# A gated FFT and MLP mix: the second forward product merged into one 512-wide product, first pieces loaded in halves, and a new order of work

## The chip, the cores and the metric

The kernel runs on one core of a Trainium2 chip. Its time is the device time of one execution in microseconds; of several runs the median is given. The engines are TensorE (PE, with its weight loads as PEld), VectorE (DVE), ScalarE (ACT), GpSimd (POOL) and SyncE (SP); the queues of SP, ACT and POOL issue DMAs.

## The reference

For x of 2048 positions by 512 features, in float32:

```python
g = sigmoid((x * gate_w).sum(-1, keepdims=True))
a = irfft2(rfft2(x) * (w_r + 1j * w_i), s=(2048, 512))
b = gelu(x @ w1 + b1) @ w2 + b2          # 512 -> 1792 -> 512
out = g * a + (1 - g) * b
```

## The kernel before

**Number format.** Every matmul operand is split into a high and a low part (type fp32r, names ending in `h` and `l`): ACT or DVE casts the high part, DVE subtracts it to get the low one. A product is then three matmuls, high x high, low x high and high x low, summed in PSUM. All matmuls are issued at line 530, from the helper `mm`.

**The MLP.** The 2048 positions are four column groups c of 512, the 1792 hidden features fourteen groups f of 128. `mlp(half, c)` does seven of the f: the up product `ph` (12 matmuls of 512 columns, line 1105), gelu on ACT (1106), a split of the result into `g_..h` and `g_..l`, and the down product `po` over four output groups q (line 1137). For the very first tile, f=0 of c=0, the up product goes in two groups of 256 columns (lines 1093 to 1103), so that it can begin with two of four input pieces: x0 and x4, then x8 and x12. Input tiles are `xf` (x0, with the gate's weights behind it; issued by ACT, line 606) and `xr` (x4, x8, x12 and later ones; by SP, line 588). `split_1` makes `mxh` and `mxl` of them (649, 650). The weights are `war` and `wbr`, split into `wa..` and `wb..`.

**The FFT.** The 2048 positions are 16 residues j by 128 rows. For each j, `forward(j)` folds the 512 features into even and odd sums (`eo`, `cl`), splits them, multiplies them by a cosine and sine table `cf` (first forward product `pd`, per cosine and sine half c: two matmuls of 260 columns and two of 130), casts and subtracts the result into `xh` and `xl`, and multiplies those along the 128 rows by the table `tf` (second forward product `py`). Sixteen `Y[j]` are then combined by radix-4 steps on DVE, filtered, and transformed back (`pz`, `pa`). The outputs of both branches are weighted with the gate and added, partly by accumulating DMAs.

**The second forward product before.** The halves c = 0 and c = 1 have a PSUM tile of 258 columns each (line 747). For c = 1 the table is read 64 columns further on, for which ACT copies 64 of its columns behind its end (710). So there are six matmuls of 258 columns a group j. ACT copies the first tile to `pys` (757); DVE adds it to the second into `Y[j]` part 0 (758). Part 1 is the difference with its 64-partition halves swapped: for the first four j DVE writes both halves (767), for the twelve in `BY_ACT` DVE subtracts once (761) and ACT moves the halves (764).

**Start.** DVE clears a tile, eleven 512-wide matmuls on it keep PE busy (`warm`), ACT loads its function table (595), and the first DMAs go out: x0 by ACT; by SP the first weight, x4, x8 and x12, each in one piece of 256 KB.

**Order.** `add` makes a step for each instruction or small group, with engine, estimated cost and the tiles that it reads and writes. `schedule` (line 219) plays the steps through as a list schedule: on each engine the ready step with the least rank goes next, if its tiles find a slot (`slots`, `most`: at most three `py` tiles). The ranks come from the table `RANKS` (line 342), one a step. The steps are emitted in that order, so each engine's queue is fixed when the kernel is built, and runs in order.

Of the kernel before, what the change touches and what calls it, by code (L numbers as in the profile page):

```python
# [11 lines left out]
F32 = mybir.dt.float32  # L12
# [5 lines left out]
P = 128  # L18
# [97 lines left out]
SPARE = 0.4  # L116
LATE_X = 1
# [55 lines left out]
class Graph:  # L173
# [5 lines left out]
    def add(self, eng, cost, lag, emit, reads=(), writes=(), rank=1):  # L179
# [10 lines left out]
        for x in reads:  # L190
            b, ps = parts(x)
            for p in ps:
                if b.wrote[p] is not None:
                    deps.add(b.wrote[p])
                b.read[p].append(s)
            if b not in s.bufs:
                s.bufs.append(b)
# [258 lines left out]
def tile_kernel(ctx: ExitStack, tc: tile.TileContext, xt, w1, w2, b1, b2, x0g, wf, wrev, out, consts):  # L456
# [37 lines left out]
    def c_pe(n, k=1):  # L494
        return k * (n / 2400 + 0.0135) + 0.005
# [102 lines left out]
    def warm():  # L598
        for _ in range(11):
            mm(none.ap(), zero.ap(), bcast(zero.ap(), 4), True, True)  # L600
# [6 lines left out]
    for j in NORD[1:4]:  # L607
        XF[j] = load_x(j)
# [682 lines left out]
```

## Time and profile before

| what | value |
|---|---|
| median of 3 runs | 372.84 us (372.68 to 372.93) |
| profiled execution, span from first to last instruction | 370.8 us |
| time of a run outside such a span (372.84 - 370.8) | 2.04 us |
| granted TensorE clock, mean | 0.999 |
| PE matmuls | 1838 |
| DVE, ACT, POOL instructions | 691, 454, 54 |

The page gives the profiled execution's span and no other time of it, so times of runs are compared with spans by way of the 2.04 us. In the rows of the profile a group of instructions has its line, engine, operation, and output<-input tiles with buffer numbers left out; matmuls overlap, so the step from one start to the next is what a matmul costs PE, and its own duration is longer. A bracket at the end of a row holds the idle time of the engine before it, and what ended it. In rows by window, the columns are the window, its length, each engine's busy time with its number of instructions, the granted clock, the DMA engines' busy share, and GB/s.

### The profile page before, as it was taken

The numbers are of one execution on the slowest core, as the hardware profiler recorded it, in microseconds if no ns is written. First come the engines' busy times: TensorE is split into PE (matmuls) and PEld (weight loads), VectorE is DVE, ScalarE is ACT, GpSimd is POOL, SyncE is SP. The second block draws the span as 40 slices with busy tenths as digits, with TensorE's granted clock in tenths as the row PEclk, the third lists the DMA queues.
The fourth block names the chain that finished last, engine by engine and source line by source line (L and its number), as shares of the span: only waits on it lengthen the run. The fifth ranks groups of instructions, "written<-read, shape, count | busy, mean of one in ns | idle before, by whom it ended". The sixth has DMA issues, their size and how long they took to land.

```text
span 370.8 us, 5565 instructions
## 1 busy us (share of the span) xinstructions
PE 365.1 (98%) x1838; PEld 309.9 (84%) x1838; DVE 327.5 (88%) x691; ACT 229.6 (62%) x454; POOL 44.1 (12%) x54
## 2 busy tenths in 40 slices
PE   8999999999999999999999999999999999999995
PEld 6888888888888888888888888888888888888885
DVE  4999999999999789999999999588849696789996
ACT  5776587976678735375367213894697549457830
POOL 0000000000000002021032020001403222221031
PEclk9999999999999999999999999999999999999999
DMA  8962899425954216479289762318968999736268
GB/s 276 389 194 73 257 282 342 147 71 151 289 173 141 77 23 170 142 157 256 72 214 267 225 120 55 57 25 291 209 130 112 211 285 187 130 88 139 88 85 198
DMA packets 50868, 62.99 MB, mean 170 GB/s; under 512 B 4656, under 2 KB 31344, under 8 KB 50064
## 3 DMA queue, kind: packets, MB, share of 16 engines
q1 hardware_dynamic: 43496, 49.54, 41.3%
q0 software_dynamic: 7200, 12.85, 23.1%
q8 instruction: 14, 0.23, 0.2%
q10 hardware_dynamic: 144, 0.26, 0.2%
q14 instruction: 14, 0.11, 0.1%
HBM read 38.64 MB, written 23.73 MB: 168 GB/s over the span
## 4 chain that ended last, share of the span: by engine, by line
PE 95%; DVE 1%; DMA 1%; issue 0%; ACT 0%; SPq 0%; DVEq 0%
PE ph L530 41%; PE po L530 40%; PE pz L530 4%; PE pd L530 4%; PE py L530 3%; PE pa L530 3%; DMA xr<-in_xt 1%; DVE uv L1002 0%; DVE y L1021 0%; SPq L588 0%; DVE y L1024 0%; DVE mxl L650 0%; DVE o L1168 0%; ACT mxh L649 0%; ACT od L999 0%
## 5 line engine op out<-in xcount | busy, mean ns | idle before, releaser
L1106 ACT ACTIVATE ph<-ph,b1t 128x512 f32<-128x512 f32 x56 | 36.9, 659 | 41.5 <-PE ph L530 39.9
L949 ACT ACTIVATE sw<-y,al 64x512 f32<-64x512 f32 x32 | 23.0, 722 | 2.2 <-DVE y L812 1.6
L908 DVE TENSOR_TENSOR m<-y,wf 128x514 f32<-128x514 f32 x32 | 20.8, 689 | 0.2
L956 DVE SCALAR_TENSOR_TENSOR pq<-y,al,sw 128x256 f32<-128x256 f32 x32 | 14.4, 481 | 5.9 <-ACT sw L952 5.5
L521 POOL DMA_DIRECT2D bacc<-o x12 | 10.5, 877 | 73.2 <-ACT o L1155 60.2
L521 POOL DMA_DIRECT2D wa7l<-in_w x1 | 1.0, 1017 | 141.0 <-ACT wa7l L582 141.0
L1155 ACT ACTIVATE o<-po 128x512 f32<-128x512 f32 x12 | 7.1, 595 | 15.9 <-PE po L530 15.8
L1152 ACT ACTIVATE o<-po,b2t 128x512 f32<-128x512 f32 x16 | 10.7, 686 | 7.6 <-PE po L530 7.5
L1002 DVE TENSOR_TENSOR uv<-pa,od 128x512 f32<-128x512 f32 x16 | 10.6, 685 | 3.6 <-ACT od L999 3.5
L764 ACT ACTIVATE y<-pys 64x257 f32<-64x257 f32 x24 | 10.0, 418 | 5.2 <-DVE pys L761 4.8
L530 PE MATMUL pd<-cf,eoh 128*128 128x260 f32 x64 | 12.7, 285 | 0.0
L688 DVE TENSOR_TENSOR eo<-xr 128x256 f32<-128x256 f32 x30 | 12.0, 418 | 0.0
L530 PEld LDWEIGHTS pd<-cf,eoh 128*128 128x128 f32 x64 | 10.6, 189 | 1.5 <-issue 0.2
L999 ACT ACTIVATE od<-pa 128x512 f32<-128x512 f32 x8 | 4.8, 599 | 10.2 <-PE pa L530 9.9
L952 ACT ACTIVATE sw<-y 1x512 f32<-1x512 f32 x16 | 10.1, 629 | 0.4
L530 PE MATMUL pd<-cf,eol 128*128 128x130 f32 x64 | 10.3, 253 | 0.0
L702 DVE TENSOR_TENSOR xr<-eo 128x256 f32<-128x256 f32 x24 | 9.8, 418 | 0.1
L530 PEld LDWEIGHTS pd<-cf,eol 128*128 128x128 f32 x64 | 9.6, 189 | 0.1
L649 ACT ACTIVATE mxh<-xm 128x512 fp32r<-128x512 f32 x12 | 6.9, 623 | 3.7 <-PE ph L530 3.7
L650 DVE TENSOR_TENSOR mxl<-xm,mxh 128x512 fp32r<-128x512 f32 x12 | 7.8, 686 | 1.2 <-ACT mxh L649 1.2
L705 DVE TENSOR_TENSOR eol<-xr,eoh 128x512 fp32r<-128x512 f32 x12 | 8.3, 688 | 0.2
L1046 DVE SCALAR_TENSOR_TENSOR ba<-gb,ba 128x512 f32<-128x512 f32 x12 | 8.1, 685 | 0.3 <-DMA ba<-bacc 0.3
(713 smaller groups left out, 1353.6 us busy)
## 6 DMA issues: line engine op xcount, KB each, us to landing
wf<-in_wf SPq DMA_DIRECT2D x16, 257.0 KB, 4.9
bacc<-o SPq DMA_DIRECT2D x16, 256.0 KB, 3.3
xr<-in_xt SPq DMA_DIRECT2D x15, 256.0 KB, 3.5
war<-in_w SPq DMA_DIRECT2D x14, 256.0 KB, 3.5
wbr<-in_w SPq DMA_DIRECT2D x14, 256.0 KB, 3.5
xm<-in_xt SPq DMA_DIRECT2D x12, 256.0 KB, 4.3
bacc<-o POOLq DMA_DIRECT2D x12, 256.0 KB, 4.0
ba<-bacc SPq DMA_DIRECT2D x12, 256.0 KB, 3.2
```

What stands on the lines that cost most here:

```text
L521: return add("pool", kb / 150, 3.4, lambda: nc.gpsimd.dma_start(dst(), src(), accum_op=ALU.add), reads, writes, rank)
L530: pe.matmul(ps, w, x, start=start, stop=stop)
L688: v(lambda s=s, op=op: vec.tensor_tensor(eo.ap()[:, s], x.ap()[:, 0:2], x.ap()[:, 2:4], op=op), 256, [x], [(eo, s)], FEED)
L702: v(lambda k=k, op=op: vec.tensor_tensor(quarter(cl, k), eo.ap()[:, :, 0], eo.ap()[:, :, 1], op=op), 256, [eo], [(cl, k)] if j % 4 == 0 or ...
L764: a(lambda o=o, i=i: act.activation(Y[j].ap()[o:o + HP, 1], pys.ap()[i:i + HP, 1], AF.Copy), 257, [(pys, 1)], [(Y[j], 1 + k)], 0, more=0.1)
L908: v(lambda mk=mk, k=k, y=y, w=w: vec.tensor_tensor(mk.ap(), y.ap(), w.ap()[:, k:k + 1, :ND].to_broadcast([P, 2, ND]), op=ALU.mult), 514, [ ...
L949: a(lambda sw=sw, y=y, o=o, i=i: act.activation(sw.ap()[o:o + HP], y.ap()[i:i + HP, ::-1, :HD], AF.Copy, scale=al.ap()[i:i + HP, 0:1]), 51 ...
L952: a(lambda sw=sw, y=y, j=j: act.activation(sw.ap()[HP:HP + 1], y.ap()[HP:HP + 1, ::-1, :HD], AF.Copy, scale=math.cos(math.pi * j / NJ)), 5 ...
L956: v(lambda sw=sw, pq_=pq_, y=y, j=j, k=k, op=op: vec.scalar_tensor_tensor(pq_.ap()[:, k], y.ap()[:, k, :HD], al.ap()[:, 1 + j:2 + j], sw.a ...
L1002: v(lambda i=i, op=op: vec.tensor_tensor(uv.ap()[:, :, i], ps.ap()[:, 0], od.ap(), op=op), 512, [ps, od], [(uv, i)], 2)
L1106: a(lambda f=f, ps=ps: act.activation(ps.ap(), ps.ap(), AF.Gelu_apprx_tanh, bias=b1t.ap()[:, f:f + 1]), 600, [b1t], [ps], 0.9 if half else ...
L1152: a(lambda o=o, ps=ps, q=q: act.activation(o.ap(), ps.ap(), AF.Identity, scale=-1.0, bias=b2t.ap()[:, q:q + 1]), 600, [b2t, ps], [o])
```

## The change

- The second forward product has one PSUM tile of 2 x 256 columns and one table position: three matmuls of 512 columns a group j. The table needs no copied columns.
- `py` is read out otherwise. ACT writes four pieces of 64 partitions straight into `Y[j]`, halves swapped, two of them negated; DVE then adds `py` twice in place. `pys` and `BY_ACT` are gone. Two columns that nobody writes now are cleared once by DVE (`clear`).
- x0, x4 and the first up weight come in two halves each, as two DMAs. Their splits go by halves; x4's cast moves from ACT to DVE. f=1 of c=0 also goes in two 256-column groups, and the first group of f=0 in two steps by halves of the features. Three of the eleven zero matmuls are gone.
- The planner orders reads of one PSUM tile by different engines behind each other, allows two `py` tiles, estimates a short matmul at no less than 0.112, and has a new `RANKS` table.

```diff
 SPARE = 0.4
+ZEROS = 8
 LATE_X = 1
...
                     deps.add(b.wrote[p])
+                if b.tag in ("pf", "pm"):
+                    deps.update(r for r in b.read[p] if r.eng != eng)
                 b.read[p].append(s)
...
 RANKS = (
-    -149, 43, 217, 3, 143, 100, 150, 574, 1118, 447, 437, 885, 624, 1856, 1001, 866, 832, 912, 1753, 1799, 1869, 396,
+    -1294, -1681, 554, 214, -655, -102, -843, 97, 121, -1398, 751, 2949, 1182, 1225, 695, 1380, 2704, 1217, 1445, 764,
...
-    most = {("pm", "ph"): 2, ("pm", "po"): 2, ("pm", "po0"): 1, ("pm", "py"): 3, ("t2k", "pq"): 2}
+    most = {("pm", "ph"): 2, ("pm", "po"): 2, ("pm", "po0"): 1, ("pm", "py"): 2, ("t2k", "pq"): 2}
...
     def c_pe(n, k=1):
-        return k * (n / 2400 + 0.0135) + 0.005
+        return k * max(n / 2400 + 0.0135, 0.112)
...
-    def load_x(j, tag="xr", rank=FEED):
-        x = buf(tag, [P, NQ, P], F32, f"x{tag[1:]}{j}")
-        dma(lambda: sp.dma_start(x.ap(), xt[j]), 512 if j == NORD[1] else 256, [], [x], j / 100 if tag == "xr" and j in NORD[:4] else rank, 2.45 if j in NORD[:4] else None)
+    def load_x(j, tag="xr", rank=FEED, parts=1):
+        x = buf(tag, [P, NQ, P], F32, f"x{tag[1:]}{j}", parts=parts)
+        n = NQ // parts
+        for k in range(parts):
+            dma(lambda k=k: sp.dma_start(x.ap()[:, k * n:(k + 1) * n], xt[j][:, k * n:(k + 1) * n]), 256 / parts, [], [(x, k)],
+                j / 100 if tag == "xr" and j in NORD[:4] else rank, 2.45 if j in NORD[:4] else None)
         return x
 
+
+    def clear():
+        vec.memset(yy.ap()[:, :, 0, P:P + 1], 0.0)
+        vec.memset(yy.ap()[:, :, 1, HD:], 0.0)
 
     zero, none = buf("hid", [P, P], F32R, "zero"), buf("pm", [P, 4, P], F32, "none", pool=pp)
     add("vec", 0.3, 0.1, lambda: vec.memset(zero.ap().bitcast(F32), 0.0), [], [zero], 0)
...
       -1).table = "gelu"
 
     def warm():
-        for _ in range(11):
+        for _ in range(ZEROS):
             mm(none.ap(), zero.ap(), bcast(zero.ap(), 4), True, True)
 
-    add("pe", 4.75, 0.1, warm, [zero], [none], 0)
-
-    x0 = buf("z", [P, NQ + 1, P], F32, "xf0")
+    add("pe", 0.427 * ZEROS - 0.4, 0.1, warm, [zero], [none], 0)
+
+    x0 = buf("z", [P, NQ + 1, P], F32, "xf0", parts=2)
     XF = {0: x0}
-    dma_act(lambda: act.dma_start(x0.ap().rearrange("p a b -> p (a b)")[:, :NQ * P + NQ], x0g), 258, [], [x0])
+    add("vec", 0.2, 0.1, clear, [], Y, 0.7)
+    for k, (u, w) in enumerate(((0, HD), (HD, D + NQ))):
+        dma_act(lambda u=u, w=w: act.dma_start(x0.ap().rearrange("p a b -> p (a b)")[:, u:w], x0g[:, u:w]), 129, [], [(x0, k)])
     for j in NORD[1:4]:
-        XF[j] = load_x(j)
+        XF[j] = load_x(j, parts=2 if j == NORD[1] else 1)
...
-        return [buf("xhl", [P, NQ, 4, P], F32R, f"mx{k}{half}{c}", parts=4) for k in "hl"]
+        return [buf("xhl", [P, NQ, 4, P], F32R, f"mx{k}{half}{c}", parts=8) for k in "hl"]
+
+    def px(b, j1, ks=(0, 1)):
+        return [(b, 2 * j1 + k) for k in ks]
 
     def split_1(xx, x, j1, rank=2):
         h, l = xx
-        a(lambda: act.activation(h.ap()[:, :, j1], x.ap()[:, :NQ], AF.Copy), 512, [x], [(h, j1)], rank)
-        v(lambda: vec.tensor_tensor(l.ap()[:, :, j1], x.ap()[:, :NQ], h.ap()[:, :, j1], op=ALU.subtract), 512, [x, (h, j1)],
-          [(l, j1)], rank)
+        n = len(x.wrote)
+        for k in range(n):
+            q = slice(k * NQ // n, (k + 1) * NQ // n)
+            ks = (0, 1) if n == 1 else (k,)
+            if n > 1 and j1:
+                v(lambda q=q: vec.tensor_copy(h.ap()[:, q, j1], x.ap()[:, q]), 512 // n, [(x, k)], px(h, j1, ks), rank)
+            else:
+                a(lambda q=q: act.activation(h.ap()[:, q, j1], x.ap()[:, q], AF.Copy), 512 // n, [(x, k)], px(h, j1, ks), rank)
+            v(lambda q=q: vec.tensor_tensor(l.ap()[:, q, j1], x.ap()[:, q], h.ap()[:, q, j1], op=ALU.subtract), 512 // n,
+              [(x, k), *px(h, j1, ks)], px(l, j1, ks), rank)
 
...
-        t = buf("ttab", [P, 2, P + HP], F32R, f"tf{j}", parts=2)
-        dma(lambda: raw(t.ap()[:, :, :P], tf_d[j]), 128, [], [(t, 0)])
-        a(lambda: act.activation(t.ap()[:, :, P:], t.ap()[:, :, :HP], AF.Copy), P, [(t, 0)], [(t, 1)])
-
-        def ttab(k, c):
-            return t.ap()[:, k, c * HP:c * HP + P]
+        t = buf("ttab", [P, 2, P], F32R, f"tf{j}")
+        dma(lambda: raw(t.ap(), tf_d[j]), 128, [], [t])
...
-            return some(c, [[511, 2], [1, P + 1]], 1 + k * NC)
+            return some(c, [[510 + c, 2], [1, P]], 2 + k * NC)
 
         def two(t, c):
-            return t.ap()[:, c, :NE].rearrange("p (a b) -> p a b", a=2)
-
-        xh = buf("z", [P, 2, 512], F32R, f"x{j}h", parts=2)
-        xl = buf("z", [P, 2, 512], F32R, f"x{j}l", parts=2)
+            return t.ap()[:, c].rearrange("p (a b) -> p a b", a=2)
+
+        xh = buf("z", [P, 2, HD], F32R, f"x{j}h", parts=2)
+        xl = buf("z", [P, 2, HD], F32R, f"x{j}l", parts=2)
...
-            a(lambda c=c: act.activation(two(xh, c), body(c, 0), AF.Copy), 258, [pd[c]], [(xh, c)], 0)
-            v(lambda c=c: vec.tensor_tensor(two(xl, c), body(c, 0), two(xh, c), op=ALU.subtract), 258, [pd[c], (xh, c)], [(xl, c)], 0)
-            v(lambda c=c: vec.tensor_tensor(two(xl, c), two(xl, c), body(c, 1), op=ALU.add), 258, [pd[c]], [(xl, c)], 0)
+            a(lambda c=c: act.activation(two(xh, c), body(c, 0), AF.Copy), HD, [pd[c]], [(xh, c)], 0)
             a(lambda c=c: act.activation(logit.ap()[:, n, c], some(c, [[641, 2], [NC, 2]], 0), AF.Copy), 4, [pd[c]],
               [(logit, 2 * n + c)], 0)
-
-        py = [buf("pm", [P, 512], F32, f"py{j}{c}", pool=pp, cls="py") for c in range(2)]
-        pys = t2k(f"pys{j}", cls="pys", parts=2)
-
-        def s_high(c):
+            v(lambda c=c: vec.tensor_tensor(two(xl, c), body(c, 0), two(xh, c), op=ALU.subtract), HD, [pd[c], (xh, c)], [(xl, c)], 0)
+            v(lambda c=c: vec.tensor_tensor(two(xl, c), two(xl, c), body(c, 1), op=ALU.add), HD, [pd[c]], [(xl, c)], 0)
+
+        py = buf("pm", [P, 2, HD], F32, f"py{j}", pool=pp, cls="py")
+
+        def flat(x):
+            return x.ap().rearrange("p a b -> p (a b)")
+
+        def s_high():
             for k in range(2):
-                mm(py[c].ap()[:, :NE], ttab(k, c), xh.ap()[:, c, :NE], k == 0, False)
-
-        def s_low(c):
-            mm(py[c].ap()[:, :NE], ttab(0, c), xl.ap()[:, c, :NE], False, True)
-
-        for c in range(2):
-            m(lambda c=c: s_high(c), NE, 2, [t, (xh, c)], [py[c]], 0)
-        for c in range(2):
-            m(lambda c=c: s_low(c), NE, 1, [t, (xl, c)], [py[c]], 0)
-        a(lambda: act.activation(pys.ap()[:, 0], py[0].ap()[:, 1:NE], AF.Copy), 257, [py[0]], [(pys, 0)], 0)
-        v(lambda: vec.tensor_tensor(Y[j].ap()[:, 0], py[1].ap()[:, 1:NE], pys.ap()[:, 0], op=ALU.add), 257, [py[1], (pys, 0)], [(Y[j], 0)], 0)
+                mm(flat(py), t.ap()[:, k], flat(xh), k == 0, False)
+
+        m(s_high, 512, 2, [t, xh], [py], 0)
+        m(lambda: mm(flat(py), t.ap()[:, 0], flat(xl), False, True), 512, 1, [t, xl], [py], 0)
+
+        def apart(x):
+            return bass.AP(tensor=x.tensor, offset=x.offset, ap=[list(x.ap[0]), [P + 1, 2], [1, P]])
+
         halves = ((0, HP), (HP, 0))
-        if j in BY_ACT:
-            v(lambda: vec.tensor_tensor(pys.ap()[:, 1], py[1].ap()[:, 1:NE], pys.ap()[:, 0], op=ALU.subtract), 257, [py[1], (pys, 0)],
-              [(pys, 1)], 0)
-            for k, (o, i) in enumerate(halves):
-                a(lambda o=o, i=i: act.activation(Y[j].ap()[o:o + HP, 1], pys.ap()[i:i + HP, 1], AF.Copy), 257, [(pys, 1)], [(Y[j], 1 + k)], 0, more=0.1)
-        else:
-            for k, (o, i) in enumerate(halves):
-                add("vec", 0.45, 0.1, lambda o=o, i=i: vec.tensor_tensor(
-                    Y[j].ap()[o:o + HP, 1], py[1].ap()[i:i + HP, 1:NE], pys.ap()[i:i + HP, 0], op=ALU.subtract),
-                    [(pys, 0), py[1]], [(Y[j], 1 + k)], 0)
+        for o, i in halves:
+            a(lambda o=o, i=i: act.activation(apart(Y[j].ap()[o:o + HP, 0]), py.ap()[i:i + HP, 1].rearrange("p (a b) -> p a b", a=2), AF.Copy),
+              HD, [py], [(Y[j], 0)], 0, more=0.11)
+        for k, (o, i) in enumerate(halves):
+            a(lambda o=o, i=i: act.activation(Y[j].ap()[o:o + HP, 1, :HD], py.ap()[i:i + HP, 0], AF.Copy, scale=-1.0), HD, [py], [(Y[j], 1 + k)], 0,
+              more=0.11)
+        v(lambda: vec.tensor_tensor(Y[j].ap()[:, 0, :HD], Y[j].ap()[:, 0, :HD], py.ap()[:, 0], op=ALU.add), HD, [py], [(Y[j], 0)], 0)
+        v(lambda: vec.tensor_tensor(apart(Y[j].ap()[:, 1]), apart(Y[j].ap()[:, 1]), py.ap()[:, 1].rearrange("p (a b) -> p a b", a=2), op=ALU.add),
+          HD, [py], [(Y[j], 1), (Y[j], 2)], 0)
...
-        t = buf("wr" + n, [P, D], F32, f"w{n}r{f}")
-        dma(lambda: sp.dma_start(t.ap(), (w1 if n == "a" else w2)[f]), 256, [], [t], early(n, f, 0.05) if f < FA else 2, None if n == "b" or f > 3 else 2.45 if f else 3.1)
+        two = (n, f) == ("a", 0)
+        t = buf("wr" + n, [P, D], F32, f"w{n}r{f}", parts=1 + two)
+        for k in range(1 + two):
+            u = slice(k * HD, (k + 1) * HD) if two else slice(0, D)
+            dma(lambda u=u: sp.dma_start(t.ap()[:, u], (w1 if n == "a" else w2)[f][:, u]), 256 / (1 + two), [], [(t, k)],
+                early(n, f, 0.05) if f < FA else 2, None if n == "b" or f > 3 else 2.45 if f else 3.1)
+        if two:
+            h, l = W[n, f] = [buf("w" + n, [P, D], F32R, f"w{n}{f}{k}", parts=2) for k in "hl"]
+            for k in range(2):
+                u = slice(k * HD, (k + 1) * HD)
+                v(lambda u=u: vec.tensor_copy(h.ap()[:, u], t.ap()[:, u]), HD, [(t, k)], [(h, k)], EARLY - 0.1)
+                v(lambda u=u: vec.tensor_tensor(l.ap()[:, u], t.ap()[:, u], h.ap()[:, u], op=ALU.subtract), HD, [(t, k), (h, k)], [(l, k)],
+                  EARLY - 0.1)
+            return
...
-            if half == c == f == 0:
-
+            if half == c == 0 and f < 2:
                 for n in range(2):
-                    def some(k, l, first, last, n=n, f=f, ps=ps):
-                        for q in range(NQ):
+                    def some(k, l, qs, first, last, n=n, f=f, ps=ps):
+                        for q in qs:
                             mm(ps.ap()[:, 2 * n * P:(2 * n + 2) * P], W["a", f][k].ap()[:, q * P:(q + 1) * P],
                                xx[l].ap()[:, q, 2 * n:2 * n + 2].rearrange("p a b -> p (a b)"), first and q == 0,
                                last and q == NQ - 1)
 
+                    hs = 2 if n == f == 0 else 1
                     for z, (k, l) in enumerate(((0, 0), (1, 0), (0, 1))):
-                        m(lambda k=k, l=l, z=z, some=some: some(k, l, z == 0, z == 2), 256, 4,
-                          [W["a", f][k], *((xx[l], 2 * n + i) for i in range(2)), *((ps, i) for i in range(n))], [(ps, n)])
+                        for g_ in range(hs):
+                            qs = range(g_ * NQ // hs, (g_ + 1) * NQ // hs)
+                            w = W["a", f][k]
+                            m(lambda k=k, l=l, z=z, some=some, qs=qs: some(k, l, qs, z == 0, z == 2), 256, len(qs),
+                              [(w, g_) if hs == 2 else w, *(p for i in range(2) for p in px(xx[l], 2 * n + i, (g_,) if hs == 2 else (0, 1))), *((ps, i) for i in range(n))],
+                              [(ps, n)])
             else:
...
-    BY_ACT = NORD[4:]
```

More of the change, by code (lines that the diff above doesn't have):

```diff
@@ L658, in keep_x @@
                 dma(lambda k=k, b=b, j=j: sp.dma_start(xs[c, k].ap()[:, :, j], b.ap()[:, :, j].bitcast(F32)), 256,
-                    [(b, j), *late], [(xs[c, k], j)], 6)
+                    [*px(b, j), *late], [(xs[c, k], j)], 6)
     def load_mx(half, c):
```

216 rows, old and new, of the table RANKS are left out of this document.

## The prediction

> **What bounds the kernel now.** I read the page first: busy time, the slices, and the chain that ended last.
>
> ```profile
> span 370.8 us, 5565 instructions
> PE 365.1 (98%) x1838; PEld 309.9 (84%) x1838; DVE 327.5 (88%) x691; ACT 229.6 (62%) x454; POOL 44.1 (12%) x54
> DVE  4999999999999789999999999588849696789996
> PE 95%; DVE 1%; DMA 1%; issue 0%; ACT 0%; SPq 0%; DVEq 0%
> ```
>
> TensorE is the chain (95%); DVE is nearly as full over the first third. A busy PE may hide waits, so next come its windows: the four stretches of the start, then the rest in one.
>
> ```profile
> 1.06:4.64 3.58, 3.58 (x9) 1.00 0.75 240
> 4.64:5.68 1.04, 0.95 (x4) 1.00 1.05 323
> 5.68:9.48 3.80, 3.59 (x24) 1.00 1.07 378
> 9.48:12.23 2.75, 2.75 (x15) 1.00 1.07 392
> 9.00:366.00 357.00, 357.00 (x1805) 303.73 (x1806) 321.94 (x677) 224.38 (x446) 43.88 (x50) 1.00 0.65 167
> ```
>
> From 9 to 366 us PE has no idle time. So time can be saved there only by giving PE less work, and before 9.48 by ending waits. The timeline of the start shows those (the brackets hold the idle time and what ended it).
>
> ```profile
> 0.74 0.41 ACTq L606 DMA_DIRECT2D xf<-in_x0g  x1
> 1.06 4.54 PE L530 MATMUL none<-zero 128*128 128x512 f32 x11 [1.06 <-DVE zero L593]
> 1.18 1.28 ACT L595 ACT_TABLE_LOAD   x1 [1.18 <-PEq L1273]
> 4.31 0.43 DVE L574 CAST wa0h<-war 128x512 fp32r<-128x512 f32 x1 [3.31 <-DMA war<-in_w]
> 4.48 0.63 ACT L649 ACTIVATE mxh<-xf 128x512 fp32r<-128x512 f32 x1 [1.80 <-DMA xf<-in_x0g]
> 5.01 1.29 ACT L649 ACTIVATE mxh<-xr 128x512 fp32r<-128x512 f32 x2
> 7.55 1.29 DVE L650 TENSOR_TENSOR mxl<-xr,mxh 128x512 fp32r<-128x512 f32 x2 [0.80 <-ACT mxh L649]
> 9.37 0.76 DVE L688 TENSOR_TENSOR eo<-xf 128x256 f32<-128x256 f32 x2
> 5.68 0.74 PE L530 MATMUL ph<-mxh,wa0h 128*128 128x256 f32 x4
> 9.48 0.40 PE L530 MATMUL ph<-mxh,wa1h 128*128 128x512 f32 x1
> 12.23 0.39 PE L530 MATMUL ph<-mxh,wa2h 128*128 128x512 f32 x1
> ```
>
> The first product waits until 5.68 for two 256 KB pieces of x, a weight, and two ACT casts in a row. `ph_0`'s 24 matmuls then take 3.80 us; their last eight wait for DVE's `mxl` of x8 and x12, which ends at 8.84. `ph_2`, which the change doesn't touch, starts at 12.23: that is the mark against which I cost the start.
>
> **The change: the merged second product.** Two stretches of PE's timeline give the step, start to start: a row of short matmuls, and the last of the down product. The chain's row of 42 gives the 512-wide step.
>
> ```profile
> 47.53 0.28 PE L530 MATMUL py<-x12l,tf 128*128 128x258 f32 x1
> 47.65 0.41 PE L530 MATMUL py<-x12h,tf 128*128 128x258 f32 x2
> 47.90 0.28 PE L530 MATMUL py<-x12l,tf 128*128 128x258 f32 x1
> 48.02 0.40 PE L530 MATMUL py<-x1h,tf 128*128 128x258 f32 x2
> 48.25 0.41 PE L530 MATMUL pd<-cf,eoh 128*128 128x260 f32 x2
> 144.12 9.52 PE po L530 x42
> 366.01 0.28 PE L530 MATMUL po<-g_13l,wb13h 128*128 128x256 f32 x1
> 366.13 0.28 PE L530 MATMUL po<-g_13h,wb13l 128*128 128x256 f32 x1
> ```
>
> Six 258-wide matmuls from 47.53 to 48.25: 0.120 us each. 9.52 / 42 = 0.2267 for 512. So a group j costs 6 x 0.120 = 0.720 before and 3 x 0.2267 = 0.680 after; 16 x 0.040 = **-0.64 us**, all on PE's path. On PE around the first group (`py`; `po` is the down product, `pd` the first forward product), before:
>
> ```order
> L530 MATMUL py_440<-x0l,tf_112 128x258
> L530 MATMUL pd_461<-cf,eoh_339 128x260 x2
> L530 MATMUL pd_455<-cf,eol_434 128x130 x2
> L530 MATMUL po_020_274<-g_3h,wb3h 128x512
> L530 MATMUL po_020_274<-g_3l,wb3h 128x512
> L530 MATMUL po_020_274<-g_3h,wb3l 128x512
> L530 MATMUL py_477<-x0h,tf_112 128x258 x2
> ```
>
> And in the changed kernel:
>
> ```order
> L533 MATMUL py_471<-x0h,tf_188 128x512 x2
> L533 MATMUL pd_476<-cf,eoh_305 128x260 x2
> L533 MATMUL pd_476<-cf,eol_443 128x130 x2
> L533 MATMUL pd_481<-cf,eoh_305 128x260 x2
> L533 MATMUL pd_481<-cf,eol_443 128x130 x2
> L533 MATMUL py_471<-x0l,tf_188 128x512
> ```
>
> The cosine and sine halves no longer go apart, and other work still stands between high and low part, as cover for the split. The Trainium skill ("TensorE: Matmul & The Clock Gate", Back-to-back issue gap) puts the warm gap at N/2.4 + 2.5 ns; by that the merge would save 12.6 ns a group, 0.2 us in all, and the rows' 0.120 for 258 columns differ from its 0.110.
>
> Reading `py` out moves from DVE to ACT. The rows, by tile:
>
> ```profile
> L757 ACT ACTIVATE pys<-py x16: 370/387/389, 32.4 to 115.6; 128x257 f32<-128x257 f32 x16
> L764 ACT ACTIVATE y<-pys x24: 417/418/421, 51.6 to 117.3; 64x257 f32<-64x257 f32 x24
> L758 DVE TENSOR_TENSOR y<-py,pys x16: 414/418/427, 35.5 to 116.4; 128x257 f32<-128x257 f32 x16
> 45.00:55.00 10.00, 8.47 (x23) 1.00 0.93 285
> ```
>
> ACT has four 64-partition writes a group, about 4 x 0.40 = 1.6 us. Before, it had 0.39, the table copy (about 0.3), and for twelve groups 0.84 more: it gains some 0.9 us for four groups and nothing much for twelve. DVE keeps two adds of 0.42 and loses a third pass in the first four groups. None of it is on PE's path while PE has other products queued; ACT's fullest ten microseconds (last row) hold 8.47, with one of the four heavier groups: 9.4. Taken at 0; at worst the rival below. `py` may hold two PSUM slots instead of three, one bank each where a group took two: no cost.
>
> **The split of f=1.** Twelve 512-wide matmuls become twenty-four 256-wide ones: 24 x 0.12 (366.01 to 366.13) - 12 x 0.2267 = **+0.16 us**.
>
> **The start.** PE before (`ph_0`, `ph_1` are hidden groups 0 and 1):
>
> ```order
> L530 MATMUL none<-zero 128x512 x11
> L530 MATMUL ph_0_127<-mxh_110,wa0h 128x256 x4
> L530 MATMUL ph_0_127<-mxh_110,wa0l 128x256 x4
> L530 MATMUL ph_0_127<-mxl_125,wa0h 128x256 x4
> L530 MATMUL ph_0_127<-mxh_110,wa0h 128x256 x4
> ```
>
> And now:
>
> ```order
> L533 MATMUL none<-zero 128x512 x8
> L533 MATMUL ph_0_120<-mxh_103,wa0h 128x256 x2
> L533 MATMUL ph_1_142<-mxh_103,wa1h 128x256 x4
> L533 MATMUL ph_1_142<-mxh_103,wa1l 128x256 x4
> L533 MATMUL ph_0_120<-mxh_103,wa0h 128x256 x2
> L533 MATMUL ph_0_120<-mxh_103,wa0l 128x256 x2
> L533 MATMUL ph_1_142<-mxl_107,wa1h 128x256 x4
> ```
>
> The first matmul needs three halves, 384 KB instead of 770 KB; the 386 KB less are about 1.0 us at 378 GB/s, and one cast goes to DVE beside ACT's. So 4.7 to 4.8 us, where the eight zeros end. The next products need all of x0, and its second half is issued by ACT behind the table load, at about 2.7 instead of 0.74 (1.18 + 1.28 + 0.2); with xf's 3.74 us from issue to use (0.74 to 4.48) less half its bytes it lands at 5.6 to 6.1. Two matmuls run, then PE mostly waits until about 6.5.
>
> What then holds PE is DVE. Its queue before, up to the low parts of x12 and x8 (`xr_98`, `xr_96`):
>
> ```order
> L574 CAST wa0h<-war_78 128x512
> L617 TENSOR_TENSOR gs<-xf_76 128x2 x2
> L577 TENSOR_TENSOR wa0l<-war_78,wa0h 128x512
> L650 TENSOR_TENSOR mxl_125<-xf_76,mxh_110 128x4x128
> L650 TENSOR_TENSOR mxl_125<-xr_82,mxh_110 128x4x128
> L620 TENSOR_TENSOR gq<-gs 128x2
> L650 TENSOR_TENSOR mxl_125<-xr_98,mxh_110 128x4x128
> ```
>
> Now, behind the first two casts (`xr_78` is x4):
>
> ```order
> L672 TENSOR_TENSOR mxl_107<-xf_76,mxh_103 128x2x128
> L669 CAST mxh_103<-xr_78 128x2x128
> L1090 TENSOR_TENSOR wa0l<-war_85,wa0h 128x256
> L629 TENSOR_TENSOR gs<-xf_76 128x2 x2
> L580 TENSOR_TENSOR wa1l<-war_96,wa1h 128x512
> L1089 CAST wa0h<-war_85 128x256
> L672 TENSOR_TENSOR mxl_107<-xf_76,mxh_103 128x2x128
> L672 TENSOR_TENSOR mxl_107<-xr_78,mxh_103 128x2x128
> ```
>
> Pieces are halved, `wa1l` has moved ahead, and x12 and x8 follow three rows later. Here `gs` waits for x0's second half, and `wa1l` with all that PE needs next is queued behind it. Steps: 512-wide 0.60 (1.29 less one of 0.69), 256-wide 0.34 (0.76 less 0.42), a half cast about 0.2 as an estimate from 0.43 for the whole. From the first half's arrival near 3.9 (256 KB less on the wire than at 4.48, 0.68 us at 378 GB/s): four casts of halves 0.8, six 256-wide subtractions 2.04, three 512-wide ones 1.8, a sum `eo` 0.34, the small ones 0.3: 5.3 us, and 0.3 of waiting, so 9.5 against 8.84. After it PE has 4 + 12 matmuls, 1.92 us: `ph_2` at 11.4. Counted on PE instead: 42 matmuls from 6.5 at 0.12, with 0.2 for restarts: 11.7. I take 11.7: **-0.5 us**. Bounds: -0.9 (all that the first matmul gains) and +0.3 (the second half at the late end, and each wait kept).
>
> **The end.** After the last `pa`, 39 matmuls of 0.12 us follow in both, and DVE does the same ten passes; only the two last halves' order on DVE and SP alternates. 0, within 0.2 either way. The rest of the new order: PE has the same work and 0 waits now; 0, and up to +1 where a product comes before its operand.
>
> **Sum.** -0.64 + 0.16 - 0.5 = -0.98: the span goes from 370.8 to 369.8, and the median of the runs, 2.04 above the span, from 372.84 to **371.9 us**.
>
> **The rivals.** *Clock not warm.* Zeros start at 0.427 us each, and the last of them are faster:
>
> ```profile
> 4.21 0.63 PE L530 MATMUL none<-zero 128*128 128x512 f32 x1
> 4.64 0.49 PE L530 MATMUL none<-zero 128*128 128x512 f32 x1
> 4.96 0.63 PE L530 MATMUL none<-zero 128*128 128x512 f32 x2
> ```
>
> The full rate came at about 4.7, while zeros ran. Eight zeros end just there, and then PE is mostly idle. If PE stays slow up to 9.5, 256-wide ones take half of 0.427, 0.213: some 20 of them lose 0.093, 1.9 us, of which the waits before 6.5 and DVE's chain cover about 0.6. Start +0.8 instead of -0.5: 373.2, no change. For it: only 3.6 us of zeros; against: that was enough, and the switch came within them. The same page of the Trainium skill (Part 1, The HAM clock gate) says that the warm-up is a time, about 3.4 us, in a window that runs freely; by that rule this rival is open, and the trace agrees with the length. 0.1.
>
> *The start gains nothing*, because x0's late half keeps DVE: only the products' -0.48: 372.4, no change. 0.17.
>
> *ACT becomes the bound, slower.* In ACT's queue the four writes stand together, and the next group's `x8h` cast behind them. Each such group then holds up that cast, and with it the next `py`, by 1.6 - 0.4 = 1.2 us. PE waits where the products between a group's `pd` and its `py` are fewer than this (five 512-wide ones). One uncovered group eats the gain; from two on it is slower: 2.4 - 0.98 = +1.4, 374.3. Against: ACT's 62%. It, or another misplaced wait of the new order: 0.1.
>
> *The merge doesn't shorten PE*, since a weight load is hidden under 512 columns anyway: PEld's 84% speaks for it, the 0.120 step against. 372.5: within the case of no change, 0.03.
>
> **How the numbers follow.** The forecast has 0.6: 371.9, by itself from 371.2 to 372.3. A measurement of this kernel can tell 0.2%, 0.75 us: faster is below 372.1, slower above 373.6. Faster: nine tenths of the forecast's 0.6, 0.54. Same: its rest and three rivals, 0.06 + 0.1 + 0.17 + 0.03 = 0.36. Slower: 0.1. The range takes in the forecast's bounds and the rivals without change, and leaves out the slower one and the two ends of the start's bounds: 371.1 to 373.4.
>
> **What would show it.** In the trace after: `py` three steps of 0.227; the first matmul near 4.75 and `ph_2` at 11.7; steps of 0.12 in `ph_0` from the first (0.21 if the clock is cold); no PE idle from 12 to 365. PE idle ended by ACT's `x..h` or `y` rows in 30 to 75 us would make me wrong; so would `ph_2` past 12.2.

## The result, and the profile after

The changed kernel is slower: five runs took 374.93 to 376.59 us, against a median of 372.76 us for six runs of the kernel before on the same chip. The ratio is 1.0083, 95% interval 1.0068 to 1.0098, so +3.1 us. A sixth run of the changed kernel, 454.23 us at a granted clock of 0.755, was disturbed and is left out. The forecast was 371.9 us, the range 371.1 to 373.4.

The page of the profiled execution (376.32 us) shows PE as full as before, and a chain of waits with a DMA in it that before's chain lacked: `ywas`, 1%. The `xr` of the start was there before.

```profile
span 374.5 us, 5533 instructions
PE 366.9 (98%) x1799; PEld 309.1 (83%) x1799; DVE 327.3 (87%) x695; ACT 233.1 (62%) x462; POOL 44.1 (12%) x54
PE 93%; DVE 2%; DMA 2%; ACT 1%; issue 0%; SPq 0%; ACTq 0%
PE ph L533 40%; PE po L533 40%; PE pz L533 4%; PE pd L533 4%; PE pa L533 3%; PE py L533 3%; DMA ywas<-y 1%; DMA xr<-in_xt 1%; DVE y L1037 0%; DVE uv L1018 0%; SPq L1083 0%; DVE x13l L758 0%; DVE o L1205 0%; DVE xr L724 0%; DVE o L1200 0%
```

The timeline of PE at the start (start, duration, in brackets the idle time before) answers to the one of before:

```profile
1.06 3.78 PE L533 MATMUL none<-zero 128*128 128x512 f32 x8 [1.06 <-DVE zero L603]
4.93 0.77 PE L533 MATMUL ph<-mxh,wa0h 128*128 128x256 f32 x2
5.87 1.22 PE L533 MATMUL ph<-mxh,wa1h 128*128 128x256 f32 x4 [0.17 <-DVE mxh L669]
8.82 1.05 PE L533 MATMUL ph<-mxl,wa1h 128*128 128x256 f32 x4
9.67 0.61 PE L533 MATMUL ph<-mxh,wa0l 128*128 128x256 f32 x2
10.60 0.64 PE L533 MATMUL ph<-mxh,wa0h 128*128 128x256 f32 x4
11.07 0.64 PE L533 MATMUL ph<-mxh,wa0l 128*128 128x256 f32 x4
13.47 0.40 PE L533 MATMUL ph<-mxh,wa2h 128*128 128x512 f32 x1
```

The first product starts at 4.93, near the forecast. But four 256-wide ones take 0.85 us from 8.82 to 9.67, so 0.213 each, and 0.12 only later (10.60 to 11.07). `ph_2` starts at 13.47: 1.24 us later than before, 1.77 later than forecast.

The second loss is in the timeline of four engines between 59 and 69 us:

```profile
59.76 0.61 SPq L787 DMA_DIRECT2D ywas<-y  x1
63.95 0.38 ACT L778 ACTIVATE y<-py 64x256 f32<-64x256 f32 x1 [2.85 <-DMA ywas<-y]
64.73 0.39 ACT L755 ACTIVATE x13h<-pd 128x256 fp32r<-128x256 f32 x1
65.15 0.42 DVE L758 TENSOR_TENSOR x13l<-pd,x13h 128x256 fp32r<-128x256 f32 x1 [3.02 <-ACT x13h L755]
66.95 0.70 PE L533 MATMUL py<-x9h,tf 128*128 128x512 f32 x2 [0.59 <-DVE y L784]
68.08 0.41 DVE L784 TENSOR_TENSOR y<-y,py 128x256 f32<-128x256 f32 x1
68.54 0.73 PE L533 MATMUL py<-x13h,tf 128*128 128x512 f32 x2 [0.89 <-DVE y L784]
```

`ywas` is a transfer of two edge rows of four finished groups out of the tile y. ACT's write `y` at line 778 belongs to another group, yet it waits 2.85 us until that transfer has landed. Behind it in ACT's queue stands the cast `x13h`; DVE waits 3.02 us for that; DVE's sums that free the two `py` tiles come late; PE stops twice, 0.59 and 0.89 us.

The 3.7 us between the two spans can be split at four marks that every kernel here has. All numbers are differences of starts in the profiled executions:

| kernel | `ph_2` starts | to the last `py` | to the last matmul | to the end |
|---|---|---|---|---|
| before | 12.23 | 103.41 | 250.48 | 4.66 |
| after | 13.47 | 105.23 | 250.69 | 5.14 |
| after - before | +1.24 | +1.82 | +0.21 | +0.48 |

### The profile page after: what moved, and what is told of

It reads as the page before. It is cut to its first block, busy times and chain, and to the rows that moved or that the text cites. A ratio compares the mean times of both kernels' runs of the same rounds, so it can differ in the third digit from the quotient of the medians.

```text
span 374.5 us, 5533 instructions
## 1 busy us (share of the span) xinstructions
PE 366.9 (98%) x1799; PEld 309.1 (83%) x1799; DVE 327.3 (87%) x695; ACT 233.1 (62%) x462; POOL 44.1 (12%) x54
## 4 chain that ended last, share of the span: by engine, by line
PE 93%; DVE 2%; DMA 2%; ACT 1%; issue 0%; SPq 0%; ACTq 0%
PE ph L533 40%; PE po L533 40%; PE pz L533 4%; PE pd L533 4%; PE pa L533 3%; PE py L533 3%; DMA ywas<-y 1%; DMA xr<-in_xt 1%; DVE y L1037 0%; DVE uv L1018 0%; SPq L1083 0%; DVE x13l L758 0%; DVE o L1205 0%; DVE xr L724 0%; DVE o L1200 0%
## 5 line engine op out<-in xcount | busy, mean ns | idle before, releaser
L778 ACT ACTIVATE y<-py 64x256 f32<-64x256 f32 x32 | 12.1, 377 | 4.5 <-DMA ywas<-y 3.2
L781 ACT ACTIVATE y<-py 64x256 f32<-64x256 f32 x32 | 11.9, 378 | 2.2 <-PE py L533 1.7
L533 PEld LDWEIGHTS pd<-cf,eol 128*128 128x128 f32 x64 | 10.3, 188 | 0.6
L756 ACT ACTIVATE logit<-pd 128x4 f32<-128x4 f32 x32 | 5.4, 173 | 6.6 <-PE pd L533 6.2
L524 POOL DMA_DIRECT2D out<-ba x8 | 7.2, 904 | 14.3 <-DVE pq L972 4.2
```

The source lines that it names most:

```text
L524: return add("pool", kb / 150, 3.4, lambda: nc.gpsimd.dma_start(dst(), src(), accum_op=ALU.add), reads, writes, rank)
L533: pe.matmul(ps, w, x, start=start, stop=stop)
L778: a(lambda o=o, i=i: act.activation(apart(Y[j].ap()[o:o + HP, 0]), py.ap()[i:i + HP, 1].rearrange("p (a b) -> p a b", a=2), AF.Copy), HD, ...
L781: a(lambda o=o, i=i: act.activation(Y[j].ap()[o:o + HP, 1, :HD], py.ap()[i:i + HP, 0], AF.Copy, scale=-1.0), HD, [py], [(Y[j], 1 + k)], 0, ...
```

## The experiments

The time before, run beside them, was 372.4 to 372.7 us. Each ratio is a kernel's time over that of before, and "the wait" is that for `ywas`.

**Eleven zeros**: `ZEROS = 11`, nothing else.

> The changed kernel with 11 zero products again instead of 8; all else as changed. Theory (half of the loss is TensorE's start-up rate: in the changed kernel the steps of the first products are 0.213 us per 256 columns until about 10.1 us and ph_2 starts at 13.47): with eleven zeros the early steps are 0.12 us, ph_2 starts at 11.7 to 12.3 and the kernel takes 1.2 to 1.7 us less, 374.2 to 374.7 us. Rival (the start is held by the late half of x0 and the casts behind it, on ScalarE and VectorE): ph_2 stays at 13.2 or later and the time stays at 375.6 to 376.2 us.

374.93 us, ratio 1.0076 (1.0047 to 1.0105). In the profile the 256-wide steps are 0.12 from 7.69 on, and `ph_2` starts at 12.81, between the two expectations: the rate was there, but the data were not. The median is only 0.0007 of the time before, 0.3 us, under the changed kernel's, where 1.2 to 1.7 us were expected.

```profile
5.48 0.39 PE L533 MATMUL ph<-mxh,wa0h 128*128 128x256 f32 x2
6.08 1.10 PE L533 MATMUL ph<-mxh,wa1h 128*128 128x256 f32 x4 [0.20 <-ACT wa1h L579]
7.69 0.74 PE L533 MATMUL ph<-mxh,wa1l 128*128 128x256 f32 x4 [0.51 <-DVE wa1l L580]
```

**Plain slices**: the pattern `apart` is gone, each such write is two of 128 columns.

```diff
+        pieces = ((0, 0), (P + 1, P))
         for o, i in halves:
-            a(lambda o=o, i=i: act.activation(apart(Y[j].ap()[o:o + HP, 0]), py.ap()[i:i + HP, 1].rearrange("p (a b) -> p a b", a=2), AF.Copy),
+            a(lambda o=o, i=i: [act.activation(Y[j].ap()[o:o + HP, 0, u:u + P], py.ap()[i:i + HP, 1, w:w + P], AF.Copy) for u, w in pieces],
...
```

VectorE's sum at line 784 is split in the same way.

> The changed kernel with each write into y that uses a two-row access pattern with a step of 129 (ScalarE's first two, VectorE's second sum) written as two instructions of 128 columns each with plain slices; 32 ScalarE and 16 VectorE instructions more, the same values. Theory (the patterned writes wait for the transfer of the ywas rows of other groups, and ScalarE's in-order queue passes that wait to x..h, x..l and TensorE): no ScalarE wait for ywas near 61 to 64 us, the two TensorE gaps of 0.6 and 0.9 us at 67 and 68.5 us and the late rows around them are gone, 1.8 to 2.2 us less, 373.7 to 374.1 us. Rival (ScalarE or VectorE have too much work there, or the new order does it): the added 3 to 6 us of work make the gaps wider, 376 us or more.

373.53 us, ratio 1.0022 (1.0007 to 1.0038): 0.0061 less than the changed kernel, 2.3 us. PE's two idle times there are gone, though ACT and DVE have 48 instructions more; ACT's write goes 1.1 us after the transfer's issue and waits for nothing. First the timeline, then PE's window from 65 to 70 us (length, busy PE, PEld, DVE, ACT, POOL, clock, DMA share, GB/s) of this kernel:

```profile
59.89 0.62 SPq L788 DMA_DIRECT2D ywas<-y  x1
60.99 0.44 ACT L779 ACTIVATE y<-py 64x128 f32<-64x128 f32 x2
66.08 0.61 PE L533 MATMUL py<-x9h,tf 128*128 128x512 f32 x2
66.53 0.62 PE L533 MATMUL py<-x13h,tf 128*128 128x512 f32 x2
```

```profile
65.00:70.00 5.00, 5.00 (x28) 4.15 (x27) 4.87 (x14) 3.97 (x14) 0.00 (x0) 1.00 0.69 200
```

And the same window of the changed kernel:

```profile
65.00:70.00 5.00, 3.52 (x17) 2.36 (x16) 4.78 (x13) 4.22 (x10) 0.00 (x0) 1.00 0.50 150
```

From `ph_2` to the last `py` it takes 102.97 us: 2.26 less than the changed kernel. The rival, that ACT or DVE has too much work there, is out.

**Both.**

> Eleven zeros and the plain slices together. Theory (two independent losses): the sum of both gains, 3.0 to 3.9 us less than the changed kernel, 372.0 to 372.9 us, which is the time before the change or up to 0.8 us under it. Rival (one stands behind the other, so that what the start gains is lost at a later wait): no more than the larger of the two alone, 373.7 us or more.

373.04 us, ratio 1.0021 (1.0003 to 1.0039). The profiled span is 370.7, 3.8 under the changed kernel's, as the theory had it; the runs gain nothing beyond the plain slices (1.0021 against 1.0022) and stay just above the 372.0 to 372.9 us expected. `ph_2` starts at 12.40.

**Before with eight zeros**: `range(8)` for `range(11)` in the kernel before.

> The kernel before the change with 8 zero products instead of 11, nothing else. Theory (the number of zeros decides when the steps get short): the first products run at 0.21 us per 256 columns for some us, and the time goes up by 0.5 to 1.5 us, 373.3 to 374.3 us. Rival (in the changed kernel it is the halved first loads and sparse first products, not the three zeros): no change or up to 0.4 us less, 372.4 to 372.8 us.

373.43 us, ratio 1.0018 (0.9999 to 1.0037), so the time alone isn't told apart from no change. PE at its start:

```profile
1.05 3.78 PE L530 MATMUL none<-zero 128*128 128x512 f32 x8 [1.05 <-DVE zero L593]
5.96 1.22 PE L530 MATMUL ph<-mxh,wa0h 128*128 128x256 f32 x4 [1.13 <-ACT mxh L649]
7.83 1.05 PE L530 MATMUL ph<-mxl,wa0h 128*128 128x256 f32 x4
8.69 1.01 PE L530 MATMUL ph<-mxh,wa0h 128*128 128x256 f32 x4
9.54 0.64 PE L530 MATMUL ph<-mxh,wa0l 128*128 128x256 f32 x4
10.01 0.64 PE L530 MATMUL ph<-mxl,wa0h 128*128 128x256 f32 x4
```

With no other change, the steps are 0.213 until 9.5 (7.83 to 8.69 for four), and `ph_2` starts at 13.24, 1.0 later than before. So in this profile the missing zeros alone make the first products slow, in the kernel before too.

**Plain slices on ScalarE alone** (VectorE's sum keeps its pattern).

> The changed kernel (8 zeros) with plain slices for ScalarE's first two writes alone; VectorE's second sum keeps its pattern and so its wait for the ywas transfer. Theory (it is ScalarE's in-order queue that carries the wait on): most of what the plain slices on both engines gave stays, 373.6 to 374.6 us, no ScalarE wait for ywas, at most one TensorE gap under 0.6 us near 66 us. Rival (VectorE's wait for the same transfer does as much harm, since x..l and the sums stand behind it): TensorE gaps of 1.5 us or more in all near 66 us, 375.2 us or more.

373.52 us, ratio 1.0016 (1.0004 to 1.0028), as with both; near 60 us no engine is idle for `ywas`, and `ph_2` to the last `py` is 102.79. So the cost came by way of ScalarE's in-order queue; the pattern that VectorE's sum keeps costs nothing that can be seen here.

**Nine zeros, with and without fill.** The fill is six zero products of 256 columns in PE's first two waits:

```diff
+FILL = {0: 4, 1: 2}
...
+for _ in range(fill):
+    mm(ps0.ap()[:, :2 * P], zero.ap(), bcast(zero.ap(), 2), False, False)
 for q in qs:
```

> Plain slices on both engines, 9 zeros, and six zero products of 256 columns more that add nothing into the first tile, four ahead of the first wa1h products and two ahead of the first wa1l products, where TensorE waited in the kernels with 8 zeros; the values are the same. Theory (idle time of TensorE before the steps are short puts off the short steps, so filling it brings them): steps of 0.12 us from some 5 us on, ph_2 at 11.5 to 12.1, 1.2 to 1.8 us earlier than in the kernel with plain slices and 8 zeros (13.35); 372.0 to 372.7 us. Rival (the steps get short at a time of their own, or the arrival of wa1 and the late halves holds the start anyway): ph_2 at 12.6 or later, 373.0 us or more.

> Plain slices on both engines and 9 zeros, without the fill: the control of the run with nine zeros and fill. Theory (the idle time between the first real products decides, not the count): steps of 0.21 us until 9 us or later, ph_2 at 13.0 to 13.5, 373.2 to 373.8 us, as with 8 zeros. Rival (one zero more is enough): ph_2 at 12.3 or earlier, 372.5 us or less, as with the fill.

With fill 373.10 us, 1.0020 (1.0005 to 1.0035), `ph_2` at 12.47; without 373.03 us, 1.0014 (1.0003 to 1.0024), `ph_2` at 12.22. With nine zeros, then, idle time between the first products does not put off the short steps, against my theory. Both times are above what was expected for a quick start: 372.7 us at most with fill, 372.5 without. PE without the fill:

```profile
1.06 4.21 PE L533 MATMUL none<-zero 128*128 128x512 f32 x9 [1.06 <-DVE zero L603]
5.06 0.63 PE L533 MATMUL ph<-mxh,wa0h 128*128 128x256 f32 x2
5.81 0.81 PE L533 MATMUL ph<-mxh,wa1h 128*128 128x256 f32 x4
7.47 0.40 PE L533 MATMUL ph<-mxh,wa0h 128*128 128x256 f32 x2
```

One zero more, 4.0 instead of 3.6 us of unbroken work, was enough here. Over all profiles: the nine with nine to eleven zeros have steps of 0.12 from 8 us at the latest, and three with eight zeros have steps of 0.21 until 9.3 to 10.1 us. The fourth with eight zeros, plain slices on ScalarE alone, went otherwise. Its start, and a window of it (length, busy PE, granted clock, DMA share, GB/s):

```profile
5.18 0.47 PE L533 MATMUL ph<-mxh,wa0h 128*128 128x256 f32 x2 [0.46 <-DVE wa0h L1090]
6.20 0.81 PE L533 MATMUL ph<-mxh,wa1h 128*128 128x256 f32 x4 [0.54 <-ACT wa1h L579]
7.25 0.74 PE L533 MATMUL ph<-mxh,wa1l 128*128 128x256 f32 x4 [0.25 <-DVE wa1l L580]
7.83 0.59 PE L533 MATMUL ph<-mxh,wa0h 128*128 128x256 f32 x2
8.65 1.05 PE L533 MATMUL ph<-mxl,wa1h 128*128 128x256 f32 x4
9.51 0.63 PE L533 MATMUL ph<-mxh,wa0l 128*128 128x256 f32 x2
```

```profile
7.83:11.20 3.37, 3.37 (x18) 0.51 0.95 335
```

Four products take 0.58 us from 7.25 to 7.83, the first step being longer after the wait, but 0.86 from 8.65 to 9.51. So eight zeros did bring the full rate there; it was lost again behind three waits of PE, for 3.4 us, and `ph_2` starts only at 13.88. What decides after eight zeros, their number or the idle time behind them, is therefore not settled; from nine on, no profile shows either loss at the start.

**Whole first pieces** (eleven zeros, plain slices; x0, x4 and the first weight each by one transfer, casts in halves):

> Plain slices, 11 zeros, and the first pieces (x0, x4 and the first weight) each loaded by one whole transfer again; the casts stay in halves, in the order of the changed kernel. Theory (the halves bring nothing once the zeros end at 5.5 to 5.9 us and wa1 arrives after 5.2 us): the first real product between 5.5 and 6.2, ph_2 within 0.4 us of the 12.40 with halves, 372.6 to 373.4 us. Rival (the halves do save loading time): first product and ph_2 later by 0.6 us or more, 373.6 us or more.

373.06 us, ratio 1.0004 (0.9994 to 1.0015); `ph_2` at 12.36 against 12.40 with halves, whose ratio is 1.0021 (1.0003 to 1.0039). The halves bring nothing.

**The pattern in the kernel before**: ScalarE's writes of y's second half get `apart`; column 128 is left out, and cleared once at the start.

```diff
-                a(lambda o=o, i=i: act.activation(Y[j].ap()[o:o + HP, 1], pys.ap()[i:i + HP, 1], AF.Copy), 257, [(pys, 1)], [(Y[j], 1 + k)], 0, more=0.1)
+                a(lambda o=o, i=i: act.activation(apart(Y[j].ap()[o:o + HP, 1]), apart(pys.ap()[i:i + HP, 1]), AF.Copy), 257, [(pys, 1)], [(Y[j], 1 + k)], 0, more=0.1)
...
```

> The kernel before the change, with the one access pattern of the change put on ScalarE's writes of y's second half (two rows of 128 with a step of 129, so column 128 is left out; it is cleared once at the start), order and counts otherwise as before. Theory (the pattern alone brings the wait for the ywas transfers of other groups, and what it costs depends on how soon after the transfer's issue the write comes): ScalarE now shows a wait for ywas, of at most 0.6 us each, because its writes come 3.7 to 5.1 us after the issue in this order; the time stays within 0.4 us of before. Rival (the wait comes from the changed values or places of the writes, not from the pattern): no wait for ywas on ScalarE at all.

373.04 us, ratio 1.0012 (1.0002 to 1.0023), 0.43 us above before and so just past the 0.4 expected. The rows give the line's wait for `ywas`: total, number of times and longest, first in this kernel, then in the changed one near 60 us.

```profile
ACT y L768 <- DMA ywas<-y: 0.3, 1, 0.3
```

```profile
ACT y L778 <- DMA ywas<-y: 2.9, 1, 2.9
```

The pattern alone brings the wait. It is 0.3 us where the write could have started 3.8 us behind the issue, 2.9 where the new order puts it 1.3 us behind. How long the transfer takes to land counts as well: a later write of the changed kernel, 1.5 us behind an issue at 79.45, waits only 0.39 us. Why the pattern, and not the plain slices, is tied to the transfer no run shows.

**Two versions.** Ten zeros, whole first pieces, plain slices on ScalarE; and the same with `"xr": 4` for 3 and a narrower `wf`.

> The version to which the runs point: plain slices on ScalarE alone, 10 zeros, whole first pieces, all else as changed. Theory (both losses are out, and the merged product's smaller sum of steps is what is left): ph_2 at 12.2 to 12.5, no TensorE gap near 66 us, 372.2 to 372.8 us, so at most 0.3 us faster than before. Rival (the new order has a third, smaller loss, the filter transfer wf that VectorE waits for near 146 us and that opens a TensorE gap near 151 us in some executions): 372.9 us or more, with such a gap in the profile.

> The version with ten zeros, whole first pieces and plain slices on ScalarE, with a fourth buffer for the tiles xr, which the filter tiles wf share (made 260 wide instead of 288 to make room); the table of ranks is the same, but the order comes out differently on every engine, so this is a version and no clean edit. Theory (what is left over the time before is mostly the filter's late landing, and the runs scatter with it): no VectorE wait for wf near 146 us, and a median of 372.0 to 372.6 us. Rival (the rest comes from elsewhere, or the other order brings waits of its own): 372.9 us or more.

The first: 373.26 us, 1.0016 (1.0000 to 1.0032), runs from 371.90 to 374.84; its profiled execution (372.04 us, span 370.2), one of its quickest, shows no gap, so neither the expected time nor the rival's gap came. The second: 407.6 us, ratio 1.0939: with the ranks kept, the one slot more changed the order on every engine, and PE is busy for 379.7 us of a span of 406.5.

No version beats the kernel before. What keeps those without the two losses 0.0004 to 0.0021 above it is not settled. Two of them show a stop of PE's weight loads (PEld) in the second part of the program that the others lack; a wait of DVE for `wf`, of 0.4 to 1.9 us in all, is in the others too. With nine zeros and fill, between 120 and 235 us:

```profile
DVE wf L921 <- DMA wf<-in_wf: 2.2, 2, 1.3
PEld po L534 <- DMA wb13l<-in_w: 1.8, 1, 1.8
PEld ph L534 <- DVE g_0l L581: 0.7, 1, 0.7
```

and with whole first pieces there:

```profile
DVE wf L920 <- DMA wf<-in_wf: 2.3, 1, 2.3
PEld ph L533 <- DVE g_0l L580: 1.5, 1, 1.5
```

That agrees with 253.04 and 252.07 us from the last `py` to the last matmul, against 250.7 in the others of the new order: PE itself stands still there for 1.7 and 1.1 us. It is seen in two of nine profiles of the new order and in none of three of the old; the run that was to remove it changed too much else.

## Why the prediction was wrong, point by point

- **Merged product, -0.64.** Right in kind: three steps for six. What can be measured, `ph_2` to the last `py` without the wait, is 102.79 to 102.98 against 103.41, so -0.4 to -0.6 with all that the new order does there. With plain slices two 512-wide `py` products start at 66.08 and the next at 66.53, so 0.225 a step, as taken. The new order, taken at 0 to +1, gives back 0.2 after it (250.7 against 250.48), apart from the wait.
- **The split of f=1, +0.16, was counted twice.** The 42 matmuls that gave `ph_2` at 11.7 already hold f=1 in its 24 short products. By the prediction's own terms the sum is -1.14, not -0.98; against the miss this is small.
- **The start, -0.5: the step that failed first.** The first product came at 4.93 as worked out, but I put the steps at 0.12. The rival "clock not warm", with 0.1, is what the profiles show: +1.24. From one profile, in which the zero at 4.64 had a faster successor, I had read that eight zeros were enough; eight end just there. That moment is not fixed: in the nine profiles with nine zeros or more, the first short step starts between 4.96 and 7.37 us, 3.9 to 6.3 us after the first zero. With eight, 3.6 us of work, it came at 9.5 to 10.3 in three profiles; in the fourth it came by 6.42, and the half rate returned behind PE's waits. The Trainium skill ("TensorE: Matmul & The Clock Gate", Part 1, The HAM clock gate) puts the change some 4 us into sustained activity, give or take 0.5; these profiles have it later and with more scatter. In the runs the zeros are worth less than in the profiles: 1.0022 against 1.0014 and 1.0021 with nine and eleven, 1.0018 for eight in the kernel before. That is between nothing and 0.7 us; how much stays open.
- Even warm the start gains nothing: `ph_2` at 12.2 to 12.8 with nine to eleven zeros, of which +0.16 is the split of f=1, against 12.23 before (11.80 in the kernel before with the pattern). That is the rival "the start gains nothing". Each zero more puts off the first product, and the whole pieces are as good as halves.
- **ScalarE's four writes, "taken at 0": the step that failed by most.** Its place was the rival "ACT becomes the bound", word for word the queue of four writes with `x..h` behind. But I priced the writes by their 0.40 us and ACT's 62%, which both held (0.38 us, 62%), and not by what they must wait for. The changed access pattern made them wait for a transfer that reads other groups' rows, and PE's stops were ended by DVE's sums behind it. That is 2.3 of the 3.1 us, shown by taking the pattern out (twice); that it alone brings such a wait is shown by putting it into the kernel before.
- **The end, 0 within 0.2**: +0.48 in that profile. DVE's chain from the first `uv` to the last `o` takes 5.40 us (365.66 to 371.06), as with whole first pieces (363.61 to 369.01); what follows is the last transfer, and with it the tail from the last matmul was 4.31 to 5.38 us over the twelve profiles, the version with four buffers apart. That is scatter, not the change.
- **What is left.** Between the forecast, 0.9 us less than before, and the result lie some 4 us. The wait is 2.3 of them, and the start 0.5 (the gain that did not come) to 1.2; the rest is open.

## What to carry to other kernels

A write that is added to a shared tile is priced by what else still reads that tile, transfers included, and by who stands behind it in its queue; its duration is the small part. A hand-made access pattern can bring waits that plain slices of the same elements do not. A table of ranks fits the set of buffers that it was made for: one buffer more with the same table gave 407.6 us here, while other counts of zeros did no such harm. A moment read from one profile, as that of the full rate at 4.7 us, should be looked up in several before a sum rests on it.

## What the runs showed of the hardware

The half rate at the start, before the first short step, doesn't show in the granted clock, and one that comes after the full rate does. Two windows of PE in the changed kernel (length, busy PE, granted clock, DMA share, GB/s), the first with steps of 0.213 and the second of 0.12:

```profile
5.87:10.10 4.23, 4.23 (x19) 1.00 1.02 350
10.10:13.47 3.37, 3.37 (x29) 1.00 1.05 398
```

And four windows of the version with four buffers, with 2.2 us of idle PE in the second:

```profile
30.00:37.00 7.00, 7.00 (x39) 1.00 0.16 56
37.60:39.80 2.20, 0.00 (x0) 1.00 0.32 78
39.80:43.40 3.60, 3.58 (x15) 0.53 0.95 283
43.50:50.00 6.50, 6.50 (x31) 1.00 0.96 274
```

An idle time of 2.2 us was enough to bring the half rate back, for 3.6 us. Shorter holes are not safe either: with plain slices on ScalarE alone, three waits of 0.46, 0.54 and 0.25 us within 2.6 us came before the half rate that shows as 0.51 from 7.83 to 11.20, while in the kernels with nine or more zeros holes of up to 0.7 us between the first products did no such harm.
